# Retention and a two-layer network in one kernel: the state's products over the four quarters of the array, its running sum in SBUF, and full-width second products for the first four tiles

## The chip, the cores and the metric

The kernel runs on one core of a Trainium2 chip. The metric is device time in microseconds (us) of one execution; the median of several runs is given. The engines are named as in the profile: PE is TensorE (matrix products), PEld its loading of weights, DVE is VectorE, ACT is ScalarE, POOL is GpSimd, SP is SyncE, which here only issues DMAs. Matrix products write to PSUM, which has eight banks of 512 float32 per partition; DVE and ACT read it, POOL doesn't.

## The reference

Retention (attention with a decay and no softmax) over 8 sequences of 576 tokens and 8 heads of 64, and then a two-layer network with an ELU on the 4608 x 512 result:

```python
scores = scale * np.matmul(q, k.transpose(0, 1, 3, 2))
gamma = 1.0 - 2.0 ** (-5.0 - np.arange(H))
rel = pos[:, None] - pos[None, :]
Dmat = np.where(rel >= 0, gamma[:, None, None] ** rel[None], 0.0)
x = np.matmul(scores * Dmat[None], v)      # heads side by side: 4608 x 512
h = x @ w_in                               # 512 x 2048
g = np.where(h > 0, h, np.exp(np.minimum(h, 0)) - 1)
out = g @ w_out                            # 2048 x 512
```

## The kernel before

**Units.** The tokens are cut into 36 units of 128. Two sequences of 576 make nine units: r = u mod 9 is 0 to 3 for the first four of the first sequence, 4 for its last 64 tokens and the first 64 of the second, 5 to 8 for the rest. The decay between two tokens is split into a factor on v (`gk`, applied by POOL in `scale_v`, L177) and one on the outputs (`gx`, applied by DVE in `put_x`, L287), so that the mask of the scores is only zeros and ones.

**One unit** runs through these steps. `load_qk` and `load_v` fetch q, k (POOL's queue, cast to bfloat16 on the way) and v (SP's queue). `turn` transposes q and k: for units below 12 on PE (L196) with copies on DVE and ACT (L197, L198), later by a DMA. `scores` (L212) makes 16 products with 64 rows, each writing 64 output partitions; `i` says which half of the rows (and which PSUM bank), `j` which half of the output partitions, so that the four quarters ("quads") of the array are used in turn. `masks` (L224, DVE) multiplies by the mask. `inter` (L240) adds the share of earlier tokens of the sequence: eight products of 64 rows with the state `sb`, where row half `i` writes output half `i`, hence two of the four quads. `state` (L257) adds k times v of this unit to the running state, which stays in the PSUM bank `ps_st` from r = 0 to 3 and from 4 to 7; `state_out` (L266, ACT) casts it to `sb` for the next unit. `intra` (L274) adds mask(scores) times v to the outputs, with 128 rows and 64 output partitions. `put_x` scales the outputs into `xt`, the network's input, with heads 2j and 2j + 1 on the two halves of the partitions of block j.

**The network.** Units are taken in groups of one to four. `ffn1` (L353) makes one PSUM bank `ph` of the hidden layer, as 128 features by up to 512 tokens: four products, then exp on ACT (L358), minus one on POOL (L360) and the ELU's max and min on DVE (L320). That last step is put off by three slots (`late`, `finish`, `tick`) and frees the bank. There are three `ph` banks. `ffn2` (L378) makes 4 of the 16 products of an output tile of 128 tokens by 512.

**Order.** The program is written in the order in which each engine takes its instructions. The start, up to the first slots of group 2, is by hand: units 0 to 3, all of group 0's and 1's first layer, and then the second layer of units 0 to 3 in eight half-width passes (`ffn2_half`, L394): columns 0 to 255 of all four tiles, then columns 256 to 511, with `turn`, `scores` and `product` of units 4 and 5 between the passes of the second round. `w_out` is loaded to fit, as two halves of its columns (L109), and `w_in` in four quarters (L105), both on POOL's queue. From then on slots alternate between `ffn1` and `ffn2`, and `stretch(u)` is put between them at due times worked out in advance: it issues `scores(u+1)`, `inter(u)`, `state(u)`, `intra(u)` on PE, then `masks(u+1)`, `put_x(u)` on DVE and `state_out(u)` on ACT.

**Banks.** `ps_h` 3, `ps_m` 1 (output tiles), `ps_s` 2 (scores), `ps_o` 1 (outputs), `ps_st` 1 (state).

Of the kernel before, what the change touches and what calls it, by code (L numbers as in the profile page):

```python
# [9 lines left out]
FP32 = mybir.dt.float32  # L10
# [3 lines left out]
ALU = mybir.AluOpType  # L14
# [3 lines left out]
def kernel(  # L18
# [9 lines left out]
    nc = tc.nc  # L28
    PSUM = bass.MemoryType.PSUM

    B, H, S, D = q.shape
    DM, DF = moe_w_in.shape
    P = 128
    HP = H // 2
# [36 lines left out]
    ps_m = ctx.enter_context(tc.tile_pool(name="ps_m", bufs=1, space=PSUM))  # L71
    ps_s = ctx.enter_context(tc.tile_pool(name="ps_s", bufs=1, space=PSUM))
    ps_o = ctx.enter_context(tc.tile_pool(name="ps_o", bufs=1, space=PSUM))
    ps_st = ctx.enter_context(tc.tile_pool(name="ps_st", bufs=1, space=PSUM))


    raws, kns = {}, {}
# [19 lines left out]

    w_in_sb = const.tile([P, KJ, DF], BF16, name="w_in_sb")
    w_out_sb = const.tile([P, NFT, DM], BF16, name="w_out_sb")
    w_in_v = moe_w_in.rearrange("(j p) f -> p j f", p=P)  # L100
    w_out_v = moe_w_out.rearrange("(f p) d -> p f d", p=P)

    def load_w_in(n):
        s = slice(n * 512, (n + 1) * 512)
        nc.gpsimd.dma_start(w_in_sb[:, :, s], w_in_v[:, :, s])  # L105

    def load_w_out(c, f0, f1):
        s = (slice(None), slice(f0, f1), slice(c * 256, c * 256 + 256))
        nc.gpsimd.dma_start(w_out_sb[s], w_out_v[s])  # L109


    kns[0] = qkpool.tile([P, 2, H, D], BF16, name="qkn", tag="qkn")
# [12 lines left out]
        nc.vector.memset(lgk[:, h : h + 1], -lg[h])  # L125
    lgx = const.tile([P, HP], FP32, name="lgx")
    for h in range(H):
        i = h % 2
        nc.vector.memset(lgx[i * D : (i + 1) * D, h // 2 : h // 2 + 1], lg[h])
    bx = const.tile([P, 1], FP32, name="bx")  # L130
    nc.vector.memset(bx, math.log(scale))

# [34 lines left out]
            nc.scalar.activation(gx[:, hp, :S], px, AF.Exp, bias=bx, scale=lgx[:, hp : hp + 1])  # L167


    qkTs, vns, scs, pts, os_, sbs, sts = {}, {}, {}, {}, {}, {}, {}  # L170

    def scale_v(u, half=None):

# [44 lines left out]
    def masks(u, i=None):  # L218
# [7 lines left out]
            m.unsqueeze(1).to_broadcast([P, (s.stop - s.start) * HP, P]), ALU.mult,  # L226
        )

    def inter(u):

        o = ps_o.tile([P, HP, P], FP32, name="o", tag="o")
        os_[u] = o
        r = u % R
        if r == 0:
            return
        n = 64 if r == 4 else P
        for hp in range(HP):
            for i in range(2):
                rows = slice(i * D, (i + 1) * D)
                nc.tensor.matmul(  # L240
                    o[rows, hp, :n], sbs[u][rows, hp], qkTs[u][rows, 0, hp, :n],
                    start=(hp == 0), stop=False, skip_group_check=True,
                )

    def state(u):

        r = u % R
        if r == 8:
            return
        if r in (0, 4):  # L250
            sts[0] = ps_st.tile([P, HP, D], FP32, name="st", tag="st")
        st = sts[0]
        rows = slice(64, P) if r == 4 else slice(0, P)
        for hp in range(HP):
            for i in range(2):
                h = 2 * hp + i
                nc.tensor.matmul(  # L257
                    st[i * D : (i + 1) * D, hp], kns[u][rows, 1, h], vns[u][rows, h],
                    start=(hp == 0 and r in (0, 4)), stop=(r in (3, 7)), skip_group_check=True,
                )  # L260

    def state_out(u):
        if u % R == 8:
            return
        s = ppool.tile([P, HP, D], BF16, name="sb", tag="sb")
        nc.scalar.copy(s, sts[0])  # L266
        sbs[u + 1] = s

    def intra(u):
        o = os_[u]  # L270
        for hp in range(HP):
            for i in range(2):
                h = 2 * hp + i
                nc.tensor.matmul(  # L274
                    o[i * D : (i + 1) * D, hp], vns[u][:, h], pts[u][:, i, hp],
                    start=(u % R == 0 and hp == 0), stop=(hp == HP - 1), skip_group_check=True,
                )

    xts = {}

    def put_x(u):
        g, i = group_of[u]
        if i == 0:
            xts[g] = xpool.tile([P, KJ, 512], BF16, name="xt", tag="xt")
        r = u % R
        s0 = P * r if r < 5 else 64 + P * (r - 5)
        nc.vector.tensor_tensor(  # L287
            xts[g][:, :, i * P : (i + 1) * P], os_[u], gx[:, :, s0 : s0 + P], ALU.mult
        )

    def stretch(u, ahead=True):

        ahead = ahead and u + 1 < NU
        if ahead:
            scores(u + 1)
        inter(u)
        state(u)
        intra(u)
        last = GROUPS[group_of[u][0]][-1] == u
        if u == 5:  # L300
            finish(2)
        if last:
            put_x(u)
        if ahead:
            masks(u + 1)
        if not last:
            put_x(u)
        state_out(u)


    gts = {}

    slot = [0]
    late = []

    def finish(n=0):

        while late and late[0][0] <= slot[0] - n:
            _, gt_, ph, m, _ = late.pop(0)
            nc.vector.scalar_tensor_tensor(gt_, ph, 0.0, m, ALU.max, ALU.min)  # L320

    def tick():
        slot[0] += 1
        finish(3)

    phs = {}

# [41 lines left out]
    def ffn2(g, s):  # L369
        it, part = divmod(s, 4)  # L370
        while late and (g, part * 4 + 3) >= late[0][4]:
            finish(slot[0] - late[0][0])
        if part == 0:
            pool, tag = ((ps_o, "o"), (ps_m, "pm"), (ps_h, "ph"))[it] if g == NG - 1 else (ps_m, "pm")
            acc[0] = pool.tile([P, DM], FP32, name="pm", tag=tag)
        pm = acc[0]
        for ft in range(part * 4, part * 4 + 4):
            nc.tensor.matmul(  # L378
                pm, gts[g, ft][:, it * P : (it + 1) * P], w_out_sb[:, ft], start=(ft == 0), stop=(ft == NFT - 1)
            )  # L380
        tick()
        if part == 3:
            ot = opool.tile([P, DM], FP32, name="ot", tag="ot")
            i0 = (GROUPS[g][0] + it) * P
            nc.scalar.copy(ot, pm)  # L385
            (nc.scalar if i0 < 8 * P else nc.sync).dma_start(out[i0 : i0 + P, :], ot)

    def ffn2_cols(u, c0, c1, bank, copy, queue):

        g, it = group_of[u]  # L390
        pool, tag = bank
        pm = pool.tile([P, c1 - c0], FP32, name="pmh", tag=tag)
        for ft in range(NFT):
            nc.tensor.matmul(  # L394
                pm, gts[g, ft][:, it * P : (it + 1) * P], w_out_sb[:, ft, c0:c1],
                start=(ft == 0), stop=(ft == NFT - 1),
            )
        ot = opool.tile([P, c1 - c0], FP32, name="oth", tag="ot")
        copy(ot, pm)  # L399
        queue.dma_start(out[u * P : (u + 1) * P, c0:c1], ot)  # L400

    def ffn2_half(u, c, bank):
        ffn2_cols(u, c * 256, c * 256 + 256, bank, A if u % 2 else V, nc.scalar)


    V, A, G = nc.vector.tensor_copy, nc.scalar.copy, nc.gpsimd.tensor_copy
# [1 line left out]
    def dummy(n, bank=(ps_m, "pm")):  # L408
        dum = bank[0].tile([P, 512], FP32, name="dum", tag=bank[1])
        for _ in range(n):  # L410
            nc.tensor.matmul(dum, warm[:, :P], warm, start=True, stop=True)

    def product(u):
        inter(u)
        state(u)
        intra(u)
        put_x(u)
        state_out(u)

    h, m = (ps_h, "ph"), (ps_m, "pm")  # L420

# [11 lines left out]
    load_v(3, queue=nc.gpsimd)  # L433
    scale_v(2)
    load_w_in(3)
    load_w_out(0, 0, 16)
    load_w_out(1, 0, 16)
    dummy(2)
    for u in range(2):
        scores(u)  # L440
        masks(u)
        if u == 0:
            make_gx(1, 2, 3)
        dummy(3)
        turn(u + 1, h, True)
        product(u)
        dummy(2)
    scores(2)
    masks(2)
# [3 lines left out]
    def f1(g, n, bank=None):  # L453
        k = 512 // (P * len(GROUPS[g]))
        ffn1(g, k * n, bank)

    o = (ps_o, "o")
    for n in range(2):
        ffn1_part(0, n, 0, 2)
    product(2)  # L460
    for n in range(2, 4):
        ffn1_part(0, n, 0, 2, m if n == 3 else None)
    two = ps_s.tile([P, 2, 512], FP32, name="ph2", tag="sc")
# [8 lines left out]
    for n in range(4, 16):  # L472
        f1(0, n, m if n % 4 == 1 else None)
        if n == 9:
            turn(3)
        if n in (9, 10):
            scale_v(3, n - 9)
        if n == 11:
            scores(3)
            masks(3, 0)  # L480
        if n == 12:
            masks(3, 1)
        if n == 13:
            product(3)
    for n in range(4):
        f1(1, n, m if n == 1 else None)
        if n == 0:
            load_v(4, nc.vector)
# [4 lines left out]
    scale_v(4)  # L493
    nc.gpsimd.tensor_copy(gx[:, :, S:], gx[:, :, 0:64])
    for u, bank in enumerate((h, h, h, m)):
        ffn2_half(u, 0, bank)
    load_qk(6)
    load_v(6, nc.vector)
    scale_v(5)
    ffn2_half(0, 1, h)  # L500
    turn(4)
    load_qk(7)
    load_v(7, nc.vector)
    ffn2_half(1, 1, h)
    scores(4)
    masks(4)
    scale_v(6)
    ffn2_half(2, 1, h)
    product(4)
    turn(5)  # L510
    load_qk(8)
    load_v(8, nc.vector)
    ffn2_half(3, 1, m)
    scores(5)
    masks(5)
    f1(2, 0)
    f1(2, 1)
    turn(6)
# [63 lines left out]
    u = NU - 1  # L582
    ffn2_cols(u, 0, 256, (ps_s, "sc"), V, nc.scalar)
    ffn2_cols(u, 256, 384, h, A, nc.scalar)
    ffn2_cols(u, 384, 512, (ps_st, "st"), V, nc.sync)
# [1 line left out]
_INS = ['q', 'k', 'v', 'moe_w_in', 'moe_w_out']  # L587
_OUTS = [((4608, 512), 'float32')]
# [25 lines left out]
```

## Time and profile before

| | |
|---|---|
| median of 4 runs | 315.38 us (315.16 to 315.95) |
| the profiled execution | 315.34 us |
| its span, first to last instruction | 313.6 us |
| granted TensorE clock in it | 0.999 |
| PE busy, 0 to 26 us of the span | 22.23 us |
| PE busy, 200 to 250 us | 49.68 us |
| DVE busy, 70 to 90 us | 13.77 us |
| DMA | 39.55 MB, mean 126 GB/s over the span and 187 GB/s from 0 to 26 us |
| `state` on PE, records | 256, from 9.9 to 259.5 us |
| `inter` on PE, records | 256, from 12.7 to 267.1 us |

The busy times are those of the profile's windows. A product's record lasts longer than the time it holds the array, since products are pipelined: the chain of work that ended last, in order of time, gives what each piece adds, and that view is the one to read for PE. A few product records are missing from the trace, and the chain then shows a short piece of "issue". "Idle before" in the timeline, in square brackets, is the time in which the engine stood still before the instruction, with what ended it.

### The profile page before, as it was taken

What the parts mean: (1) busy time and instruction counts of PE and PEld (TensorE: products, weight loads), DVE (VectorE), ACT (ScalarE), POOL (GpSimd) and SP (SyncE); (2) the same over time, 40 slices, a digit from 0 to 9 for tenths busy, and PEclk for the clock granted to TensorE, in tenths of its full rate; (3) what the DMA queues carried; (4) which work ended last, traced back from release to release, by engine and by line L of the source; (5) the groups of instructions that cost most, each with busy time, mean ns of one, the idle gap of its engine ahead of it and who ended that gap; (6) DMA issues with size and microseconds to landing.
All of it is one profiled execution on the core that took longest, in us unless ns stands there. A gap on an engine that the chain in (4) does not pass through costs nothing.

```text
span 313.6 us, 7519 instructions
## 1 busy us (share of the span) xinstructions
PE 303.0 (97%) x2992; PEld 173.8 (55%) x3028; DVE 172.5 (55%) x279; ACT 130.6 (42%) x243; POOL 200.2 (64%) x288
## 2 busy tenths in 40 slices
PE   8898999999999999999999999999999999999995
PEld 3475988776765555554454444444444444444444
DVE  4667435757756667655565655565555555434300
ACT  5465215355444543444444443434434443344311
POOL 8985894968977777797777666766664433333300
PEclk9999999999999999999999999999999999999999
DMA  9999999997999999999899999999996200001111
GB/s 158 191 207 199 193 215 166 203 143 67 132 113 184 144 121 194 125 123 195 98 162 128 128 131 131 134 135 132 133 132 86 69 33 36 34 33 41 62 68 68
DMA packets 149219, 39.55 MB, mean 126 GB/s; under 512 B 137600, under 2 KB 145152, under 8 KB 149184
## 3 DMA queue, kind: packets, MB, share of 16 engines
q0 software_dynamic: 79248, 13.64, 55.8%
q1 hardware_dynamic: 67920, 23.14, 40.0%
q10 hardware_dynamic: 2016, 2.29, 2.3%
q8 instruction: 23, 0.38, 0.5%
q14 instruction: 12, 0.10, 0.1%
HBM read 36.70 MB, written 9.44 MB: 147 GB/s over the span
## 4 chain that ended last, share of the span: by engine, by line
PE 87%; DMA 6%; DVE 2%; POOL 2%; issue 1%; SPq 1%; ACT 0%; DVEq 0%
PE ph L353 37%; PE pm L378 33%; PE pmh L394 6%; DMA w_in_sb<-in_moe_w_in_dram 4%; PE sc L212 4%; PE o L274 3%; PE st L257 2%; DMA rv<-in_v_dram 2%; PE o L240 2%; PE tr L196 1%; DVE pt L224 1%; DVE g L320 1%; POOL vn L177 1%; POOL qkn L94 1%; DVE xt L287 0%
## 5 line engine op out<-in xcount | busy, mean ns | idle before, releaser
L360 POOL TENSOR_SCALAR m<-e 128x512 bf16<-128x512 f32 (+1 forms) x156 | 90.7, 583 | 95.4 <-ACT e L358 91.9
L353 PE MATMUL ph<-xt,w_in_sb 128*128 128x512 bf16 (+3 forms) x792 | 141.1, 313 | 2.5 <-DMA w_in_sb<-in_moe_w_in_dram 1.0
L320 DVE SCALAR_TENSOR_TENSOR g<-ph,m 128x512 bf16<-128x512 f32 (+1 forms) x156 | 99.5, 648 | 76.1 <-POOL m L360 75.3
L358 ACT ACTIVATE e<-ph 128x512 f32<-128x512 f32 (+1 forms) x156 | 87.5, 564 | 125.8 <-PE ph L353 121.9
L378 PE MATMUL pm<-w_out_sb,g 128*128 128x512 bf16 x478 | 122.8, 380 | 1.6 <-issue 1.0
L353 PEld LDWEIGHTS <-w_in_sb 128*128 128x128 bf16 x808 | 68.9, 98 | 54.6 <-DMA w_in_sb<-in_moe_w_in_dram 1.1
L378 PEld LDWEIGHTS <-g 128*128 128x128 bf16 x496 | 47.8, 98 | 53.3 <-issue 0.3
L224 DVE TENSOR_TENSOR pt<-sc,mask 128x1024 bf16<-128x1024 f32 (+1 forms) x37 | 44.1, 1193 | 19.7 <-PE sc L212 19.4
L177 POOL TENSOR_TENSOR vn<-rv,gk 128x512 bf16<-128x512 f32 (+1 forms) x37 | 37.8, 1020 | 1.2 <-DMA rv<-in_v_dram 1.2
L94 POOL DMA_DIRECT2D qkn<-in_q_dram x39 | 35.0, 898 | 0.0
L94 POOL DMA_DIRECT2D qkn<-in_k_dram x39 | 33.4, 858 | 0.1
L287 DVE TENSOR_TENSOR xt<-o,gx 128x512 bf16<-128x512 f32 x36 | 24.7, 685 | 15.1 <-PE o L274 14.9
L385 ACT COPY ot<-pm 128x512 f32<-128x512 f32 x31 | 18.1, 585 | 14.5 <-PE pm L378 14.4
L266 ACT CAST sb<-st 128x256 bf16<-128x256 f32 x32 | 11.9, 372 | 18.3 <-PE st L257 15.5
L394 PE MATMUL pmh<-w_out_sb,g 128*128 128x256 bf16 (+1 forms) x176 | 18.3, 263 | 0.0
L394 PEld LDWEIGHTS <-g 128*128 128x128 bf16 x176 | 15.7, 98 | 1.9
L212 PEld LDWEIGHTS <-qkT 64*64 64x64 bf16 x576 | 9.2, 106 | 13.5 <-issue 11.0
L212 PE MATMUL sc<-qkT 64*64 64x128 bf16 x576 | 15.1, 222 | 0.6 <-ACT qkT L198 0.2
L274 PE MATMUL o<-pt,vn 128*64 128x128 bf16 x288 | 14.3, 221 | 0.0
L399 DVE COPY oth<-pmh 128x256 f32<-128x256 f32 (+1 forms) x6 | 2.4, 402 | 18.0 <-PE pmh L394 18.0
L240 PE MATMUL o<-qkT,sb 64*64 64x128 bf16 (+1 forms) x256 | 12.3, 214 | 0.0
L198 ACT COPY qkT<-tr 128x512 bf16<-128x512 bf16 x12 | 7.0, 584 | 8.8 <-DVE rv L83 3.1
(41 smaller groups left out, 93.7 us busy)
## 6 DMA issues: line engine op xcount, KB each, us to landing
rv<-in_v_dram SPq DMA_DIRECT2D x31, 256.0 KB, 4.9
out_dram<-ot SPq DMA_DIRECT2D x27, 256.0 KB, 2.3
qkn<-in_q_dram POOLq DMA_DIRECT2D x31, 128.0 KB, 5.3
qkn<-in_k_dram POOLq DMA_DIRECT2D x31, 128.0 KB, 5.3
w_in_sb<-in_moe_w_in_dram POOLq DMA_DIRECT2D x4, 512.0 KB, 10.5
w_out_sb<-in_moe_w_out_dram POOLq DMA_DIRECT2D x2, 1024.0 KB, 18.2
out_dram<-oth ACTq DMA_DIRECT2D x9, 128.0 KB, 4.7
rv<-in_v_dram SPq DMA_DIRECT2D x8, 128.0 KB, 5.7
```

The costliest lines, as they stand in the source:

```text
L94: nc.gpsimd.dma_start(kns[u][p0 : p0 + n, c], (q, k)[c][b, :, s0 : s0 + n, :].rearrange("h p d -> p h d"))
L177: nc.gpsimd.tensor_tensor(vns[u][:, h0:h1], raws[u][:, h0:h1], gk[:, u % R, h0:h1].unsqueeze(2).to_broadcast([P, h1 - h0, D]), ALU.mult,)
L212: nc.tensor.matmul(sc[j * 64 : (j + 1) * 64, i, hp], t[r, 1, hp, j * 64 : (j + 1) * 64], t[r, 0, hp], start=(hp == 0), stop=(hp == HP - 1) ...
L224: nc.vector.tensor_tensor(pts[u][:, s].rearrange("p i h t -> p (i h) t"), scs[u][:, s].rearrange("p i h t -> p (i h) t"), m.unsqueeze(1).t ...
L274: nc.tensor.matmul(o[i * D : (i + 1) * D, hp], vns[u][:, h], pts[u][:, i, hp], start=(u % R == 0 and hp == 0), stop=(hp == HP - 1), skip_g ...
L287: nc.vector.tensor_tensor(xts[g][:, :, i * P : (i + 1) * P], os_[u], gx[:, :, s0 : s0 + P], ALU.mult)
L320: nc.vector.scalar_tensor_tensor(gt_, ph, 0.0, m, ALU.max, ALU.min)
L353: nc.tensor.matmul(ph[:, i * n : (i + 1) * n], w_in_sb[:, j, f : f + P], xts[g][:, j, :n], start=(j == 0), stop=(j == KJ - 1), skip_group_ ...
L358: nc.scalar.activation(e[:, w], ph[:, w], AF.Exp)
L360: nc.gpsimd.tensor_scalar(m[:, w], e[:, w], -1.0, 1.0, ALU.add, ALU.mult)
L378: nc.tensor.matmul(pm, gts[g, ft][:, it * P : (it + 1) * P], w_out_sb[:, ft], start=(ft == 0), stop=(ft == NFT - 1))
L394: nc.tensor.matmul(pm, gts[g, ft][:, it * P : (it + 1) * P], w_out_sb[:, ft, c0:c1], start=(ft == 0), stop=(ft == NFT - 1),)
```

## The change

- `inter` uses all four quads. The output of head h = 4b + 2a + i now stands on partition half b, in bank i, columns 128a on; row half i is unchanged. `ps_o` has two banks (`[P, 2, 512]`), each half used for outputs.
- The rows of `w_in` are laid out to match (heads 4b + j on half b of block j), by two DMAs of 64 partitions per quarter. `gx`, `put_x` and `intra` follow the new layout.
- `ps_st` is gone. The state's products of unit u go into the free half of one of the banks of unit u - 1's outputs, each unit's products by themselves; in `stretch(u)` they are those of u + 1 and come after `intra(u)`.
- The running state is kept as float32 in SBUF (`sum`): DVE adds the unit's products to it one slot after the stretch, and ACT casts it one slot later. For r = 3 and 7 DVE writes the bfloat16 state at once. For units 0 to 3 ACT first copies the products to SBUF (`state_aside`).
- The second layer of units 0 to 3 runs at full width: features 0 to 7 of all four tiles, then features 8 to 15 (`ffn2_part`), and `w_out` is loaded as two halves of its rows.
- The last of the final three column passes takes a bank of `ps_o`.

The diff, cut to its core:

```diff
-    w_in_v = moe_w_in.rearrange("(j p) f -> p j f", p=P)
+    w_in_v = moe_w_in.rearrange("(b j p) f -> b p j f", b=2, j=KJ)
...
-        nc.gpsimd.dma_start(w_in_sb[:, :, s], w_in_v[:, :, s])
+        for b in range(2):
+            nc.gpsimd.dma_start(w_in_sb[b * 64 : b * 64 + 64, :, s], w_in_v[b, :, :, s])
...
+    def load_w_out(f0, f1):
+        nc.gpsimd.dma_start(w_out_sb[:, f0:f1], w_out_v[:, f0:f1])
...
+    def outputs(o):
+        return o[:, :, 0:256].rearrange("p i (a t) -> p a i t", a=2)
...
-        o = ps_o.tile([P, HP, P], FP32, name="o", tag="o")
+        o = ps_o.tile([P, 2, 512], FP32, name="o", tag="o")
...
-        for hp in range(HP):
-            for i in range(2):
-                rows = slice(i * D, (i + 1) * D)
-                nc.tensor.matmul(
-                    o[rows, hp, :n], sbs[u][rows, hp], qkTs[u][rows, 0, hp, :n],
-                    start=(hp == 0), stop=False, skip_group_check=True,
-                )
+        for a in range(2):
+            for b in range(2):
+                for i in range(2):
+                    rows = slice(i * D, (i + 1) * D)
+                    nc.tensor.matmul(
+                        o[b * D : (b + 1) * D, i, a * P : a * P + n], sbs[u][rows, 2 * b + a],
+                        qkTs[u][rows, 0, 2 * b + a, :n],
+                        start=(a == 0), stop=False, skip_group_check=True,
+                    )
...
+        sts[u] = os_[u - 1][:, 1 if r == 4 else 0, 256:512].rearrange("p (c d) -> p c d", c=HP)
...
+    def state_out(u, cast_later=False):
+        r = u % R
+        if r == 8:
+            return
+        s = ppool.tile([P, HP, D], BF16, name="sb", tag="sb")
+        sbs[u + 1] = s
+        if r in (3, 7):
+            nc.vector.tensor_tensor(s, sts[u], sums[u - 1], ALU.add)
+            return
+        sums[u] = ppool.tile([P, HP, D], FP32, name="sum", tag="sum")
+        if r in (0, 4):
+            nc.vector.tensor_copy(sums[u], sts[u])
+        else:
+            nc.vector.tensor_tensor(sums[u], sts[u], sums[u - 1], ALU.add)
+        if cast_later:
+            todo.append((slot[0] + 1, lambda: nc.scalar.copy(s, sums[u])))
+        else:
+            nc.scalar.copy(s, sums[u])
+
+    def state_aside(u):
+        c = ppool.tile([P, HP, D], FP32, name="stc", tag="stc")
+        nc.scalar.copy(c, sts[u])
+        sts[u] = c
...
+                for b in range(2):
+                    h = 4 * b + 2 * a + i
+                    nc.tensor.matmul(
+                        o[b * D : (b + 1) * D, i, a * P : (a + 1) * P], vns[u][:, h], pts[u][:, i, 2 * b + a],
+                        start=(u % R == 0 and a == 0), stop=(a == 1), skip_group_check=True,
+                    )
...
     def stretch(u, ahead=True):
...
         inter(u)
-        state(u)
         intra(u)
+        if ahead:
+            state(u + 1)
...
-        state_out(u)
+        if ahead:
+            todo.append((slot[0] + 1, lambda: state_out(u + 1, True)))
...
     def tick():
         slot[0] += 1
         finish(3)
+        while todo and todo[0][0] <= slot[0]:
+            todo.pop(0)[1]()
...
+    def ffn2_part(u, f0, f1, bank):
+        g, it = group_of[u]
+        if f0 == 0:
+            pool, tag = bank
+            acc[u] = pool.tile([P, DM], FP32, name="pm", tag=tag)
+        for ft in range(f0, f1):
+            nc.tensor.matmul(
+                acc[u], gts[g, ft][:, it * P : (it + 1) * P], w_out_sb[:, ft], start=(ft == 0), stop=(ft == NFT - 1)
+            )
+        if f1 == NFT:
+            ot = opool.tile([P, DM], FP32, name="ot", tag="ot")
+            (A if u % 2 else V)(ot, acc[u])
+            nc.scalar.dma_start(out[u * P : (u + 1) * P, :], ot)
...
     def product(u):
         inter(u)
-        state(u)
         intra(u)
         put_x(u)
-        state_out(u)
...
         if n == 12:
             masks(3, 1)
+            state(3)
+            state_aside(3)
         if n == 13:
             product(3)
+            state_out(3)
...
     for u, bank in enumerate((h, h, h, m)):
-        ffn2_half(u, 0, bank)
+        ffn2_part(u, 0, 8, bank)
...
-    ffn2_half(0, 1, h)
+    ffn2_part(0, 8, 16, None)
...
     scores(4)
+    state(4)
     masks(4)
+    state_out(4)
```

## The prediction

> **What bounds the kernel now.** I read the page first, for the engine at the limit and the chain that ended last.
>
> ```profile
> PE 303.0 (97%) x2992; PEld 173.8 (55%) x3028; DVE 172.5 (55%) x279; ACT 130.6 (42%) x243; POOL 200.2 (64%) x288
> ...
> PE 87%; DMA 6%; DVE 2%; POOL 2%; issue 1%; SPq 1%; ACT 0%; DVEq 0%
> PE ph L353 37%; PE pm L378 33%; PE pmh L394 6%; DMA w_in_sb<-in_moe_w_in_dram 4%; PE sc L212 4%; PE o L274 3%; PE st L257 2%; DMA rv<-in_v_dram 2%; PE o L240 2%; PE tr L196 1%; DVE pt L224 1%; DVE g L320 1%; POOL vn L177 1%; POOL qkn L94 1%; DVE xt L287 0%
> ```
>
> The tensor engine (PE) is the bound: 97% busy and 87% of the chain. PE time removed after the start is kernel time; work on any other engine is free until PE waits for it. The chain in order of time then gives the pieces of one stretch (start, length, what):
>
> ```profile
> 72.42 0.22 PE o L240 x8
> 72.64 0.34 PE o L274 x8
> ...
> 217.84 0.86 PE pm L378 x4
> 218.71 0.35 PE sc L212 x16
> 219.06 0.22 PE o L240 x8
> 219.28 0.25 PE st L257 x8
> 219.52 0.23 PE o L274 x8
> ```
>
> Four 512-column products take 0.86, so 128 columns take 0.216/4 = 0.054 us. The state's share of the outputs (L240) takes 0.22 for eight products of 128 columns: four times 0.054, two abreast. The intra products take 0.23 after the state products, of the same shape, but 0.34 straight after L240 (at 72.64): a change from 64-row to 128-row products costs 0.11. Third, the timeline of the start:
>
> ```profile
> 14.55 0.82 POOL L105 DMA_DIRECT2D w_in_sb<-in_moe_w_in_dram  x1
> ...
> 26.03 1.48 PE L353 MATMUL ph<-xt,w_in_sb 128*128 128x384 bf16 x8 [0.98 <-DMA w_in_sb<-in_moe_w_in_dram]
> ...
> 34.64 1.44 POOL L94 DMA_DIRECT2D qkn<-in_q_dram  x2
> ```
>
> The last quarter of w_in, issued at 14.55, lands just before 26.03, and PE sat idle for 0.98 before it. PE work moved ahead of 25 us is covered by that idle time. Last, the timeline where VectorE (DVE) holds PE up:
>
> ```profile
> 109.94 1.23 DVE L224 TENSOR_TENSOR pt<-sc,mask 128x1024 bf16<-128x1024 f32 x1 [0.79 <-PE sc L212]
> ...
> 111.08 0.68 DVE L287 TENSOR_TENSOR xt<-o,gx 128x512 bf16<-128x512 f32 x1
> ...
> 111.38 1.70 PE L353 MATMUL ph<-xt,w_in_sb 128*128 128x384 bf16 x8
> 111.67 1.01 DVE L320 SCALAR_TENSOR_TENSOR g<-ph,m 128x384 bf16<-128x384 f32 x2
> ```
>
> Eight such products take 1.46 to 1.47 at 105.91, 108.07 and 113.78, but 1.70 here: PE waits 0.24 for a bank that DVE frees after mask and xt. The like stands at 119.26 (1.74, so 0.27).
>
> **The state's share over four quads.** The scores show what four abreast cost. In the timeline they start at 218.64 and L240 at 218.88: 0.24 for 16 products, 0.06 for each four. Eight products of L240 then take two steps of 0.054, 0.11, in place of 0.22: 0.11 saved per unit. If they don't overlap further, it is nothing; I take 0.11, because shape, columns and the alternation of rows and output halves become those of the scores, which the trace shows. L240 is run by 32 units. Units 1 and 2 run before 25 us, where PE waits for w_in anyway. Four units (r = 4) have 64 columns, and at 103.21 their L240 and state products already share 0.25 of the chain, being on different quads; I count nothing there. 26 units by 0.11 give 2.9.
>
> The TensorEngine Tiling page of the Trainium skill (Instruction Overhead) speaks against this: it gives each matmul some 60 cycles, below which a narrower one is no shorter. At the 2.4 columns per ns of the rows above, that would be, by estimate, 25 ns a matmul against the 27 that L240 has, and the saving would be 26 by 8 by 0.002 = 0.4, the sum 316.0. The scores' 0.24/16 = 15 ns contradicts it.
>
> **State products one unit ahead.** The same eight products, now after intra(u) and for u+1. L240, intra and state now follow each other with one change from 64 to 128 rows, as before. Only where u+1 is a unit with r = 4 (its state products have 64 rows) is a change back added: 0.11 for each of units 13, 22 and 31, 0.3 in all (bounds 0 and 0.4). They need v scaled one unit earlier; POOL scales it two or more stretches ahead of unit 12 on, and one stretch (5 us) before that: hidden. L240 of a unit now waits for a cast a whole stretch older, so that wait is looser.
>
> **Sum and cast.** A VectorE operation on 128x256 is new for 32 units, and the cast on ScalarE falls away for r = 3 and 7. Nearest rows by shape:
>
> ```profile
> L266 ACT CAST sb<-st 128x256 bf16<-128x256 f32 x32 | 11.9, 372 | 18.3 <-PE st L257 15.5 <-PE o L274 2.7
> L399 DVE COPY oth<-pmh 128x256 f32<-128x256 f32 x5 | 2.1, 423 | 16.6 <-PE pmh L394 16.6
> ```
>
> 0.42 each, 13.5 us more on DVE, 55% to 59%. In the groups of four units (units 16 to 35) it is hidden: after the stretch at 218.64 the g that frees the bank of the next first-layer product was done at 218.2 (start 217.54, 0.69), over 3 us ahead. In the units up to 15 it is not everywhere. At the two places shown, the sum is queued between the two g operations that PE wants 0.65 apart; the second g ended 0.2 in time, so 0.42 makes 0.2 of new wait, and the 0.11 saved on PE there is lost as well. 2 by 0.3 is 0.6, and 0.1 for a transposed-query copy caught behind a sum (at 59.66 PE waited 0.24 for one): 0.7. Bounds: 0, and all 11 stretches of units 5 to 15 at 0.42 + 0.11, 5.8.
>
> **The aside copies.** In the first four units ScalarE copies the state out of the outputs' banks before L240 may write there. Three lie before 25 us. For unit 3 it comes after the exponential that now ends at 27.44, takes 0.37, and product(3), at 27.43 now, waits until about 27.8: 0.4, of which the 0.11 saved on L240 and the idle ends of neighbouring products take some; I take 0.25 (bounds 0 and 0.5). Queued behind the copy is the exponential of n = 13, on ScalarE idle 1.66 before.
>
> **Weights' DMAs.** w_in goes in eight issues for four. A 64-partition issue cost 1.44/2 = 0.72 at 34.64, so each pair costs 0.64 more than one of 0.80: 2.6 on POOL's queue, in front of the v scalings of units 0 to 2 and the loads of q, k, v of unit 3. The two w_out issues get half the pieces (1,024, like q's 0.88) and give back 0.56, so POOL's first m, now at 18.98, keeps its time. Does w_in land later? Before, v of unit 3, issued at 12.65 on the same queue, took 10.7 us, twice the usual 5; the transfers stand in line at some 200 GB/s throughout. I take 0. Bounds: 1.0 earlier (then PE's idle time vanishes) and 2.6 later.
>
> **FFN2 at full width.** 128 products of 256 columns at 1.75 per 16 (42.48 on the chain) are 14.0; 64 of 512 columns at 0.216 are 13.8: 0.15 saved (bounds 0 and 0.3). Three first-layer banks and one more are held from 33 to 47 us, in which no first-layer product runs. The first part needs half of w_out, all columns, at 33.1; its halves landed at 31.0 and 37.3, and the second is needed at 40.
>
> **Sum.** 2.9 + 0.15 - 0.3 - 0.7 - 0.25 = 1.8. The profiled execution took 315.34 (span 313.6, 1.7 around it): 313.5. The four runs' median is 315.38, so 313.6.
>
> **Rivals.** (1) Four abreast saves nothing: the change doesn't do what it says. Costs of 1.25 less 0.15 stay: 316.5. For it: L240 never ran on four quads. Against: the scores. (2) The slower one: VectorE's sum sets the pace in units 5 to 15. Place: between two g operations after a stretch. Price 0.42 + 0.11 in all 11 stretches, 5.8 in place of 0.7: 318.7. It turns the sign from 0.23 more per stretch than I take (2.5/11). For it: the two waits above, and DVE is at 13.8 of 20 us busy from 70 to 90. Against: it is idle 0.4 to 1.8 before most operations there. (3) w_in lands as late as it is issued, up to 2.6: 316.2, and no change from about 1.2 on. For it: the chain passes through POOL's issue at 14.55. Against: the line of transfers. (4) w_in lands earlier, with w_out's fewer pieces behind: up to 1.0, 312.6.
>
> **How the numbers follow.** Likeliest case 0.70, its own range 312.2 to 314.8; (1) 0.06, (2) 0.08, (3) 0.10 spread over its price, (4) 0.06. Runs of before lie within 0.25%, so under 0.2% (0.63 us) counts as no change. Faster: 0.70 less a little, and (4): 0.75. Same: most of (3) and the edge of the first: 0.12. Slower: (1), (2) and the rest of (3): 0.13. The range 312.0 to 315.7 leaves out what is left of (1), (2), (3).
>
> **What would show it.** On the chain, L240's successor at 0.11 and scores unchanged at 0.35; intra at 0.34, state 0.13; the first product after w_in still at about 26.0; FFN2 of units 0 to 3 in 13.8; the 1.70 at 111 us grown to about 2. I am wrong if the new L240 stays at 0.22, if w_in lands after 27, or if DVE stands on the chain in most stretches before 150 us.

## The result and the profile after

| | before | after |
|---|---|---|
| median | 315.36 us (61 runs, 314.68 to 316.91) | 314.54 us (37 runs, 313.77 to 317.2) |
| ratio | | 0.9977, 95% interval 0.9969 to 0.9985 |
| profiled execution | 315.34 us | 314.25 us |
| its span | 313.6 us | 312.5 us |

The change makes the kernel faster by 0.23%, some 0.7 us. The forecast was faster by 1.8 us: the sign holds, the state's share takes half its time as forecast, and over half of the gain is missing. The page of the changed kernel, its busy times and its chain:

```profile
PE 301.1 (96%) x2925; PEld 165.9 (53%) x2964; DVE 182.3 (58%) x309; ACT 127.6 (41%) x237; POOL 201.8 (65%) x292
...
PE 86%; DMA 6%; DVE 3%; POOL 3%; issue 2%; ACT 0%; POOLq 0%; DVEq 0%
```

PE is busy 1.9 us less, but its share of the chain fell from 87% to 86%, while VectorE's and POOL's each rose by a point and "issue" from 1% to 2%: some of the freed time has become waits. A stretch in the groups of four, from the chain in order of time of the changed kernel (start, length, what):

```profile
218.86 0.35 PE sc L211 x16
219.21 0.11 PE o L244 x8
219.32 0.34 PE o L299 x8
219.67 0.12 PE o L260 x8
```

It is as forecast: L244, the old L240, takes 0.11 in place of 0.22; the intra products (L299) carry the change of rows, 0.34; the state products (L260) 0.12; the scores 0.35 as before. So the gain is there, stretch by stretch. The chain's marks show where it goes. Both kernels have the product that first needs the last quarter of w_in, the second layer's first product, the scores of units 5 and 6, and the last column passes:

| mark | before | after | lost (+) or gained (-) since the mark above |
|---|---|---|---|
| last quarter of w_in used | 26.03 | 26.62 | +0.59 |
| second layer of unit 0 | 33.30 | 34.33 | +0.44 |
| scores of unit 5 | 49.44 | 50.47 | 0.00 |
| scores of unit 6 | 54.31 | 55.91 | +0.57 |
| last column passes | 306.57 | 305.98 | -2.19 |

0.24 of the 0.57 is no loss: the state products of unit 5 now stand there and are missing from a later stretch. What is lost lies in three places. And one gain stands behind the last mark: the sum of the table is -0.59, but the profiled execution is 1.09 shorter. From the last column passes to the end of the span it takes 7.0 before and 6.5 after. The 6.5 stands in all variants of the changed kernel, and in the kernel before with the full-width second layer alone; the kernel before and its other variants have 7.0. So the 0.5 comes with that part of the change; what ends sooner there is not shown, and the forecast had no term for it.

The first place is the start. POOL's first m in the kernel before:

```profile
18.98 5.15 POOL L360 TENSOR_SCALAR m<-e 128x384 bf16<-128x384 f32 x10 [1.32 <-ACT e L358]
```

and the changed kernel's timeline:

```profile
12.02 0.91 POOL L93 DMA_DIRECT2D qkn<-in_q_dram  x1 [0.57 <-DMA qkn<-in_q_dram]
13.60 0.88 POOL L93 DMA_DIRECT2D qkn<-in_k_dram  x1 [0.67 <-DMA qkn<-in_k_dram]
...
18.07 0.91 POOL L108 DMA_DIRECT2D w_out_sb<-in_moe_w_out_dram  x1 [0.36 <-DMA w_in_sb<-in_moe_w_in_dram]
19.36 0.88 POOL L108 DMA_DIRECT2D w_out_sb<-in_moe_w_out_dram  x1 [0.38 <-DMA w_in_sb<-in_moe_w_in_dram]
20.26 3.83 POOL L389 TENSOR_SCALAR m<-e 128x384 bf16<-128x384 f32 x8
...
26.62 0.81 PE L382 MATMUL ph<-xt,w_in_sb 128*128 128x384 bf16 x4 [0.33 <-DMA w_in_sb<-in_moe_w_in_dram]
```

POOL stands still four times, 2.0 us in all, before an issue, each time until an earlier DMA of its own has landed. Its first m, behind them, starts at 20.26 in place of 18.98, and PE, which had waited 0.98 for w_in, comes so late itself that it waits only 0.33, and yet starts 0.59 later. Then the chain of the changed kernel at unit 3 and after unit 5:

```profile
28.67 0.36 PE o L299 x8
29.03 0.03 issue
29.05 0.04 DVE xt L312
29.09 0.57 issue
29.66 0.41 DVE sb L275
30.08 0.48 DVE g L347
30.55 0.04 issue
30.60 3.73 PE ph L382 x64
...
52.01 0.42 DVE sum L281
52.44 0.02 issue
52.46 0.02 ACT sb L285
52.48 0.29 issue
52.77 0.60 ACT e L387
53.37 0.08 issue
53.45 0.62 POOL m L389
54.07 0.02 issue
54.10 0.73 DVE g L347 x2
54.82 0.02 issue
54.85 1.07 PE ph L382 x16
```

At unit 3 the sum (L275) stands on VectorE between xt and the g that frees PE's bank. After unit 5 a whole ladder hangs on the sum: ScalarE's cast (sb) waits for it, the exponential e stands behind the cast in ScalarE's queue, POOL's m waits for e, and g for m.

### The profile page after: what moved, and what is told of

Read it like the earlier page. It is cut to its first block, busy times and chain, and to the rows that moved or that the text cites. A ratio compares the mean times of both kernels' runs of the same rounds, so it can differ in the third digit from the quotient of the medians.

```text
span 312.5 us, 7391 instructions
## 1 busy us (share of the span) xinstructions
PE 301.1 (96%) x2925; PEld 165.9 (53%) x2964; DVE 182.3 (58%) x309; ACT 127.6 (41%) x237; POOL 201.8 (65%) x292
## 4 chain that ended last, share of the span: by engine, by line
PE 86%; DMA 6%; DVE 3%; POOL 3%; issue 2%; ACT 0%; POOLq 0%; DVEq 0%
PE ph L382 36%; PE pm L407 34%; PE pm L438 4%; PE sc L211 4%; PE o L299 4%; DMA w_in_sb<-in_moe_w_in_dram 3%; DMA qkn<-in_k_dram 3%; PE o L260 1%; POOL qkn L93 1%; PE pmh L423 1%; PE tr L195 1%; PE o L244 1%; DVE g L347 1%; DVE pt L223 1%; DVE xt L312 0%
## 5 line engine op out<-in xcount | busy, mean ns | idle before, releaser
L407 PE MATMUL pm<-w_out_sb,g 128*128 128x512 bf16 x478 | 122.8, 380 | 1.6 <-issue 0.9
L407 PEld LDWEIGHTS <-g 128*128 128x128 bf16 x496 | 47.8, 98 | 53.0 <-issue 0.3
L299 PE MATMUL o<-pt,vn 128*64 128x128 bf16 x288 | 14.9, 225 | 0.0
L438 PE MATMUL pm<-w_out_sb,g 128*128 128x512 bf16 x61 | 14.2, 380 | 0.2
L283 ACT CAST sb<-sum 128x256 bf16<-128x256 f32 x19 | 7.7, 403 | 11.8 <-DVE sum L281 8.3
L299 PEld LDWEIGHTS <-vn 128*64 128x64 bf16 x288 | 9.1, 109 | 3.1
L452 PE MATMUL dum<-warm 128*128 128x512 bf16 x26 | 8.9, 463 | 1.2 <-DVE warm L119 1.2
L260 PE MATMUL o<-vn,qkn 128*64 128x64 bf16 (+1 forms) x256 | 9.5, 196 | 0.4 <-POOL vn L176 0.4
```

Of the source, the lines that this page charges most:

```text
L299: nc.tensor.matmul(o[b * D : (b + 1) * D, i, a * P : (a + 1) * P], vns[u][:, h], pts[u][:, i, 2 * b + a], start=(u % R == 0 and a == 0), s ...
L407: nc.tensor.matmul(pm, gts[g, ft][:, it * P : (it + 1) * P], w_out_sb[:, ft], start=(ft == 0), stop=(ft == NFT - 1))
L438: nc.tensor.matmul(acc[u], gts[g, ft][:, it * P : (it + 1) * P], w_out_sb[:, ft], start=(ft == 0), stop=(ft == NFT - 1))
```

## The experiments

Each kernel ran beside the kernel before on the same chip. The start of this kernel varies from one execution to the next: in the timelines the scores of unit 4 begin between 44.99 and 46.67 in nine profiles of the changed kernel and its variants. The granted clock varies there too: in three of the fourteen profiles (unit 3's later sum, two quads again and full width alone) its mean falls to between 0.60 and 0.68, from 16 to 20 us in the first and from 12 to 16 us in the other two; in the other eleven it is 1.00 in both windows. Verdicts on the start therefore go by the runs and their intervals, those on later stretches by the trace, which repeats: from the scores of unit 6 to those of unit 35 the kernel before and its four variants take 204.56 to 204.57, the changed kernel and six of its eight variants 202.69 to 202.72. The other two change these stretches and are told below. The stretch of unit u is the time from the scores of unit u + 1, with which its products begin, to those of unit u + 2.

### The start

**The split of w_in alone.**

```diff
-        nc.gpsimd.dma_start(w_in_sb[:, :, s], w_in_v[:, :, s])
+        for b in range(2):
+            nc.gpsimd.dma_start(w_in_sb[b * 64 : b * 64 + 64, :, s], w_in_v[b * 64 : b * 64 + 64, :, s])
```

> The kernel before, with only each quarter of w_in fetched by two DMAs of 64 partitions. Theory (the split delays the start: eight issues for four on POOL's queue, and four more waits of an issue for an earlier DMA to land): POOL's first m moves from 18.98 to about 20.2 us, the last quarter lands about 0.5 us later than 25.98, the product that needs it starts at about 26.6 in place of 26.03, and the time is 0.5 to 0.7 us over the kernel before, near 316.0. Rival (the split is free, and the changed kernel loses its time later, at units 3 and 5): the product stays at 26.0 and the time at 315.4.

316.51 against 315.35, ratio 1.0042 (1.0026 to 1.0058): 1.2 us lost (0.8 to 1.8 by the interval), more than expected. POOL's m starts at 20.82. The first of the changed kernel's losses is the split's, and it is larger than the 0.59 that the trace of one execution showed. In this kernel the landing of w_in's last quarter is not what holds PE up: no product waits for it. The chain passes from the landing of an earlier part of w_in at 18.09 through the two issues of w_out, the first of which waited for it (0.39), to m at 20.82 and the g behind it.

**As many issues, split another way.** Each quarter in two DMAs of two row blocks on all 128 partitions:

```diff
-        nc.gpsimd.dma_start(w_in_sb[:, :, s], w_in_v[:, :, s])
+        for j in (0, 2):
+            nc.gpsimd.dma_start(w_in_sb[:, j : j + 2, s], w_in_v[:, j : j + 2, s])
```

> The kernel before, with each quarter of w_in fetched by two DMAs that each take two of the four row blocks on all 128 partitions: as many issues, pieces and bytes as in the split by partition halves, which cost 1.16 us. Theory (the number of issues on POOL's queue is what costs): the last quarter lands near 27 as there and the time is about 1.1 us over the kernel before. Rival (64-partition transfers are slower themselves): no cost, within 0.3 us of the kernel before.

316.2 against 315.75, ratio 1.0016 (1.0004 to 1.0029). Between the two: a cost of about 0.5 us with whole-width transfers. Its trace doesn't say why it should be less than the 1.2 before: m starts at 21.12, 0.3 later than there, again behind a wait of w_out's issue (0.51) for w_in. The two intervals, 0.1 to 0.9 and 0.8 to 1.8, just overlap.

**As many issues, with w_in whole.**

```diff
         nc.gpsimd.dma_start(w_in_sb[:, :, s], w_in_v[:, :, s])
+        nc.gpsimd.dma_start(spare[0:64, :, n * 8 : n * 8 + 8], w_in_v[0:64, :, n * 512 : n * 512 + 8])
```

> The kernel before, with each quarter of w_in in one DMA as there, and behind each a small one of 64 partitions and 256 pieces of 32 bytes into a tile that nobody reads: as many issues and waits on POOL's queue as with the split, hardly more bytes, and w_in's own transfers whole. Theory (the number of issues and of waits for earlier landings on POOL's queue is the cost): 0.5 to 1.2 us over the kernel before, as in the two split kernels. Rival (what costs is that w_in itself travels in halves): within 0.3 us of the kernel before.

318.06 against 315.6, ratio 1.0096 (1.0068 to 1.0125): 2.5 to 3 us, more than either split, with hardly a byte more. The timeline of POOL in this kernel says why:

```profile
16.13 0.89 POOL L85 DMA_DIRECT2D rv<-in_v_dram  x1 [1.56 <-DMA w_in_sb<-in_moe_w_in_dram]
...
21.42 1.15 POOL L111 DMA_DIRECT2D w_out_sb<-in_moe_w_out_dram  x1 [0.80 <-DMA w_in_sb<-in_moe_w_in_dram]
22.58 1.47 POOL L362 TENSOR_SCALAR m<-e 128x384 bf16<-128x384 f32 x3
```

POOL waits 1.56 and 0.80 for quarters of w_in to land before it may issue v of unit 3 and the second half of w_out, and its first m comes 3.6 us later than in the kernel before. So the cost is in POOL's queue, and not only in its issues' own time but in their waits. The list of the changed kernel's instructions names them: POOL's DMAs signal on eight semaphores in turn, and each issue from the ninth on waits on the one that it takes over:

```
L93 DMACopy qkn<-in_q_dram 128x8x64 [waits DMASW2_49]
L93 DMACopy qkn<-in_k_dram 128x8x64 [waits DMASW3_49]
L84 DMACopy rv<-in_v_dram 128x8x64 [waits DMASW4_49]
L176 TensorTensor vn<-rv,gk 128x512 [waits DMAHW4_49]
L105 DMACopy w_in_sb<-in_moe_w_in_dram 64x4x512 [waits DMASW5_49]
```

Eight issues for w_in use up the turn sooner. Which landing is waited for depends on the order and on the size of what is to land: in the kernel with the small issues it is a whole quarter of w_in each time, and v of unit 3 waits 1.56 for one; in the two split kernels above it does not wait. Why the two splits cost 1.2 and 0.5, if they differ, is not shown.

**Two tries to relieve the queue** in the changed kernel. The second half of w_out issued after slot n = 10:

> The changed kernel, with the second half of w_out issued after the first layer's slot n = 10 instead of at once behind the first. Theory (POOL's first m is late because the w_out issues wait for earlier DMAs to land in front of it): m starts about 1.2 us earlier than at 20.26, the product that needs the last quarter of w_in is then bound by its landing alone, 0.1 to 0.4 us earlier, and the time falls to about 314.2. Rival (the landing of w_in, late by itself, sets the end of the start): no change, 314.5.

And v of unit 3 on SP's queue:

> The changed kernel, with v of unit 3 fetched on SP's queue, after VectorE's mask of unit 0, instead of on POOL's. Theory (POOL's queue is too full at the start since w_in takes eight issues): one issue of 0.89 us and one wait less on it, w_in's last quarter is issued about 1 us earlier than at 17.08, m starts earlier too, and the time falls by 0.5 to 1.0 us, to 313.5 to 314.0. Rival (the transfers themselves are the bound, whoever issues them): no change, 314.5, or later if v's transfer holds up those of q and k of units 1 and 2.

315.56 and 315.42 against 316.07, ratios 0.9983 (0.9967 to 1.0) and 0.9983 (0.9966 to 1.0), where the changed kernel has 0.9977: no gain in either, the theories' 0.3 to 1.0 did not come. In the first the issue of w_in's last quarter itself waited for a landing, until 17.11; in the second m still began at 20.52, behind waits for w_in. One issue less was not enough to get ahead of the landings in these two kernels.

### Unit 3, unit 5 and VectorE's sums

**The sum of unit 3 two slots later.**

```diff
         if n == 13:
             product(3)
+        if n == 15:
             state_out(3)
```

> The changed kernel, with VectorE's sum of unit 3 issued two first-layer slots later (after n = 15 in place of n = 13). Theory (the sum stands between unit 3's xt and the g that frees the bank, and PE waits for that g at 30.60): the second layer of unit 0 starts 0.3 to 0.4 us earlier than at 34.33, and the time falls by as much from 314.5 to 314.1. Rival (the bank is late because of ScalarE's aside copy and the exponentials behind it, so the sum is hidden): no change, 34.3 and 314.5.

314.35 against 315.35, ratio 0.9971 (0.9957 to 0.9985), which can't be told from 0.9977. In its trace the 72 products after unit 3 run without a break, 4.98, where the changed kernel needs 5.30 from the end of the intra products (29.03 to 34.33): 0.3, as expected.

**The sum and cast of unit 5 put off.**

```diff
     masks(5)
-    state_out(5)
+    todo.append((slot[0] + 2, lambda: state_out(5, True)))
```

> The changed kernel, with unit 5's sum and cast put off by two and three slots as in the later stretches. Theory (ScalarE takes its instructions in order: the cast of unit 5 waits for the sum, the sum for the masks, and the exponentials of group 2 stand behind it, so that PE waits 0.55 us at 54.85 for a bank): the scores at 55.91 come 0.5 us earlier against those of unit 5 at 50.47 (5.44 between them, 4.87 in the kernel before), time 314.0. Rival (POOL or the transposes of unit 6 hold the bank): 5.4 between them and 314.5.

The chain of this kernel:

```profile
50.17 0.35 PE sc L211 x16
...
53.15 0.43 DVE qkT L196
53.57 0.63 DVE g L347 x2
54.20 0.02 issue
54.23 1.07 PE ph L382 x16
55.29 0.35 PE sc L211 x16
```

Neither the cast nor e stands on it any more, and the scores follow each other at 5.12 in place of 5.44. That is 0.32, all that was lost: 0.24 of the remaining 5.12 - 4.87 are the state products. The expected 0.5 had forgotten them. The runs, 314.46 against 315.35 and 0.997 (0.9951 to 0.9989), don't resolve it.

**All sums one slot later.**

```diff
-            todo.append((slot[0] + 1, lambda: state_out(u + 1, True)))
+            todo.append((slot[0] + 2, lambda: state_out(u + 1, True)))
```

> The changed kernel, with every stretch's sum one slot later (two slots after the stretch, the cast three). Theory (in the groups of three units the sum between two g operations holds a bank up): PE's products after the stretches at 111 and 121 us shrink and 0.2 to 0.5 us are saved in all, 314.2. Rival (those waits come from mask and xt alone, as in the kernel before, and the sum is hidden): nothing, 314.5.

314.91 against 316.07, ratio 0.9967 (0.9946 to 0.9988); from unit 6 to 35 202.69 against 202.72: nothing in sum. Between neighbouring scores it is three things: the stretch of unit 12 gains 0.17 and that of unit 15 gains 0.33, and the stretch of unit 10 loses 0.47. There the later sum holds up ScalarE: its cast waits for the sum, and behind the cast stands the copy ot, which frees the bank of an output tile for PE. From the chain of this kernel:

```profile
89.57 0.34 DVE sum L281
...
89.94 0.02 ACT sb L283
...
90.25 0.59 ACT ot L414
...
90.88 1.02 PE pm L407 x4
```

The 0.33 is this place on the changed kernel's chain:

```profile
118.76 0.69 DVE xt L312
119.45 1.13 DVE pt L223
120.58 0.33 DVE sb L275
120.91 0.47 DVE g L347
```

**Together, where needed.** The edits of units 3 and 5, and the later sum in two stretches alone:

```diff
-            todo.append((slot[0] + 1, lambda: state_out(u + 1, True)))
+            todo.append((slot[0] + (2 if u in (12, 15) else 1), lambda: state_out(u + 1, True)))
```

> The changed kernel, with the sum of unit 3 two slots later, the sum and cast of unit 5 put off, and in the stretches of units 12 and 15 alone the sum one slot later. Theory (the waits shown one by one add): 0.31 less up to the second layer of unit 0, 0.33 less to the scores of unit 6, 0.5 less after, 1.1 in all, 313.4. Rival (each opens another wait behind it, as the sum of unit 11 did when all were put off): 0.5 or less, 314.0.

313.23 against 315.75, ratio 0.9921 (0.9908 to 0.9935). The waits add, and this version beats both kernels, the changed one by about 0.56%. That is 1.3 to 2.3 us by the intervals; the stretches below account for 1.2 of it, and the rest, in the start if anywhere, is not shown. The chain of this kernel at units 3 and 15:

```profile
28.96 0.34 PE o L299 x8
29.31 4.99 PE ph L382 x72
...
118.00 0.69 DVE xt L312
118.69 1.13 DVE pt L223
119.82 0.48 DVE g L347
```

The sums are gone from both places. From the last quarter of w_in to the second layer it takes 7.38 (7.71 in the changed kernel, 7.27 before), between the scores of units 5 and 6 it takes 5.12 (5.44), and from unit 6 to 35 202.21 (202.72).

### Is it the quads?

**The order of the quads.** The loops over a and b exchanged, so that the two products of a quad are issued two places apart in place of four:

```diff
-        for a in range(2):
-            for b in range(2):
+        for b in range(2):
+            for a in range(2):
```

> The changed kernel, with the loops of the state's share over output halves (b) and column blocks (a) exchanged: both products on one half's two quads are issued before the other half's, so that two quads wait for themselves. Theory (what four abreast gives is steps of 0.054 us saved): three steps in place of two, the successor of L240 grows on the chain from 0.11 to 0.16 in each unit and the time by 26 x 0.054 = 1.4 us, to about 315.9. Rival (the gain came from the free banks or from the order of state and intra, not from the quads): 0.11 and 314.5 as before.

314.46 against 316.07, ratio 0.9948 (0.9932 to 0.9963). The theory's number failed: L244 stays at 0.11 and unit 6 to 35 takes 202.71. This order of the eight products costs nothing. So the rival, that the gain comes from the banks, was still open.

**Two quads again, with all else as after the change.** The intra products then write over the state's share, so that this kernel leaves it out of its result; the work on PE stays.

```diff
-                        o[b * D : (b + 1) * D, i, a * P : a * P + n], sbs[u][rows, 2 * b + a],
+                        o[i * D : (i + 1) * D, i, a * P : a * P + n], sbs[u][rows, 2 * b + a],
...
-                        start=(u % R == 0 and a == 0), stop=(a == 1), skip_group_check=True,
+                        start=(a == 0), stop=(a == 1), skip_group_check=True,
```

> The changed kernel, with the state's share written to output half i in place of b, so that row half i meets only output half i: two of the four quads, as before the change, with order, banks and counts as after it. The intra products then overwrite the outputs, so the state's share is computed and left out of the result. Theory (each quad works through its own products, and twice the quads halve the time, whatever the order): L240's successor takes 0.22 on the chain again, from the scores of unit 6 to the last column passes 25 x 0.11 = 2.7 us more than the 250.07 of the changed kernel, time near 317. Rival (the two banks are what made it faster): 0.11 and 250.1.

318.32 against 315.75, ratio 1.0083 (1.0054 to 1.0112). The chain of this kernel:

```profile
222.31 0.35 PE sc L211 x16
222.66 0.22 PE o L244 x8
222.88 0.34 PE o L299 x8
223.23 0.12 PE o L260 x8
```

0.22 is back, and unit 6 to 35 takes 205.37, 2.65 more than the changed kernel. The number of quads used decides, not the two banks, and not the order that was tried.

### Full-width second layer alone

The kernel before with `ffn2_part` and w_out in halves of its rows, as in the change.

> The kernel before, with only the second layer of units 0 to 3 at full width and w_out in halves of its rows. Theory (the prediction's term): 0.15 us saved, 315.2. Rival (the full-width products hold their banks longer or the outputs' DMAs, now later, delay the loads of units 5 to 8): the stretch from 33.3 us to the scores of unit 5, 16.14 us before, grows by 0.2 or more, 315.6.

315.54 against 315.35, ratio 1.0008 (0.9997 to 1.0018): no change that the runs can show. On its chain the second layer of unit 0 starts at 33.88 and the scores of unit 5 at 49.86: 15.98 in place of 16.14, the 0.16 of the theory. The 0.5 behind the last column passes is there too. Against them stand a second layer that starts 0.58 later in this execution (33.88 for 33.30), in which the granted clock was 0.66 from 12 to 16 us, and time outside the span: the runs of this kernel last 2.09 to 2.21 longer than their spans, those of the kernel before and of the changed one 1.72 to 1.85. In the changed kernel the 0.16 is there but spent: the transposes of unit 4 take 0.66 in place of 0.45 (42.97 to 43.63). The second half of them comes late about when k of unit 4 lands, which POOL issued a microsecond later than before.

## Why the prediction was right or wrong

The step that failed is the term for the weights' DMAs, put at nothing; behind it come the sums of units 3 and 5.

- **Four quads: right.** 0.11 per unit was the term, 0.22 to 0.11 the measurement, and two quads again cost 2.65 over units 6 to 35, where 25 units by 0.11 give 2.75. The scores' pace, the row that it was taken from, was the right one. Three units with 64 columns, counted as nothing, gained 0.06 each. The TensorEngine Tiling page of the Trainium skill (Instruction Overhead) gives each matmul some 60 cycles. Read as a time that one product after the other must take, as the prediction read it, it would have left 0.4 us; the trace does not agree with that reading: eight products in 0.11 follow each other at 14 ns. A single product's own 54 ns is above the 25 of the estimate, so as a floor for one product the figure is not tested here.
- **The added change of rows: right.** The stretches of units 21 and 30, whose state products are the 64-row ones, gain nothing (0.00); nor does that of unit 12 once its sum is moved.
- **VectorE's sums in the later stretches: right in size, in part by luck.** 0.17 and 0.33 were found at the stretches of units 12 and 15, and 0.11 of gain is missing at that of unit 14: 0.6 for 0.7. But the two places priced at 0.3 each were those of units 14 and 15. At unit 14 no sum stands on the chain; mask, xt and g set the pace there as before (110.96 to 113.26), so that PE's 0.11 buys nothing. The place at unit 12 was not named. That one could simply put all sums off was not claimed, and fails.
- **Full width: right in size**, 0.16 for 0.15, and spent elsewhere in the changed kernel. The 0.5 behind the last column passes had no term.
- **Unit 3: the wrong cause.** 0.25 was taken for ScalarE's aside copy, and the sum there was given no price. No wait for the copy stands on the chain: L244 follows the product before it without a gap (28.43). Measured on the trace: 0.44 more up to the second layer, though 0.11 was gained; 0.3 of it is the sum, the rest the state products standing between first-layer products, with a change of rows of their own (L244 takes 0.24 there). That 0.25 is not far from 0.44 is luck.
- **Unit 5: the term is missing.** Only stretches were searched for sums on the path; the hand-written part has a cast issued at once, which waits in ScalarE's order with e behind it. 0.33.
- **The weights' DMAs: the step that failed.** The prediction said that the longer issues leave POOL's first m at its time, since w_out's issues get shorter, and took 0. The issues came out below their price (1.28 per pair for 1.44), and POOL's idle time in the kernel before (0.42 and 0.46 before two scalings of v, 1.32 before m) would have taken them in. What was not seen are 2.0 us of waits of an issue for the landing of the DMA eight before it; the trace of before does not show them, since with four issues for w_in they fall on DMAs that have landed. m came 1.3 us later, the product after w_in 0.59 in the one trace, and the split alone costs 1.2 us in the runs (0.8 to 1.8). Rival (3) had the place and, with 0 to 2.6, the range of the price, but only by w_in's landing, and had 0.10.

Added up over the changed kernel: 2.19 gained after the scores of unit 6, less 0.24 that moved, leaves 1.95; 0.33 and 0.44 go at units 5 and 3, and 0.5 comes at the end: 1.68. The start takes 0.59 of it in the profiled execution, which leaves its 1.09. The runs' 0.7 us (0.5 to 1.0) leaves 0.7 to 1.2 for the start, which fits what the split alone costs. Which part of the start ends last differs: in the changed kernel's profile PE waits 0.33 for w_in's last quarter, itself issued late behind the waits in POOL's queue; with the split alone and with the small extra issues it is POOL's m, and no product waits for w_in's last quarter. How the cost divides between the two over many executions stays open, and neither relief moved the time.

The signs of being wrong that the prediction gave did not show: L244 is at 0.11, w_in lands at 26.48, and VectorE is on the chain in few stretches. None of them looks at POOL's m or at units 3 and 5.

## What to carry to other kernels

A transfer split in two can cost more than an issue on its queue: look at which landing each later issue on that queue must wait for, and at the compute queued behind. When a saving on the bound engine needs a new operation elsewhere, place each copy of that operation by what stands behind it in its engine's order; the same sum cost 0.2 to 0.3 us in four places and nothing that the trace shows in the other stretches from unit 6 on, and moving only those four gave back 1.2 us in the trace. Where the start varies by more than the effect, compare later stretches between marks of one trace, which here repeat within 0.03 us, and don't stop at the last mark: 0.5 us lay behind it.

## What was not expected of the hardware

Products on the four quads need not be issued in turn: with the two products of a quad two places apart in place of four, the eight still took 0.11 us, as if each quad had a queue of its own; that it has one is not shown. And before the change two products with different row halves wrote one bank, on different partition halves, and ran two abreast all the same (0.22 for eight, where one after the other would be eight times 0.054); writing two banks on the same two quads changed nothing (0.22).
